# A fused attention and MoE kernel on one core: its third attention unit cut into two query chunks, with MoE work between them

## The chip, the core and the metric

The kernel runs on one core of a Trainium2 chip. The core has a matrix engine, TensorE (PE in the profile, with its weight loads as PEld), which writes to eight PSUM banks; a vector engine (DVE); an activation engine (ACT); GpSimd (POOL); and a queue engine, SyncE (SP), that issues DMAs. Each engine works through its own instructions in the order of the program and waits for others by semaphores. The metric is the device time of one execution in microseconds (us), the median of several; the profile is of one further execution.

## The reference

```python
def _attn_ref(q, k, v, g_q, g_k):            # q, k, v: 8 batches, 12 heads, 448 rows, 64
    def rmsnorm(x, g):
        rms = np.sqrt(np.mean(x * x, axis=-1, keepdims=True) + 1e-06)
        return x / rms * g
    q_n, k_n = (rmsnorm(q, g_q), rmsnorm(k, g_k))
    scale = 1.0 / np.sqrt(q.shape[-1])
    scores = scale * np.matmul(q_n, k_n.transpose(0, 1, 3, 2))
    scores = scores - np.max(scores, axis=-1, keepdims=True)
    attn = np.exp(scores)
    attn = attn / (np.sum(attn, axis=-1, keepdims=True) + 1e-09)
    return np.matmul(attn, v).astype(np.float32)

def _moe_ref(x, w_in, w_out):                # 3584 x 768, 768 x 2048, 2048 x 768
    h = x @ w_in
    g = np.maximum(0.01 * h, h)
    return (g @ w_out).astype(np.float32)

# the attention's output, heads side by side, is the x of the second part
```

All inputs and the output are float32; the kernel computes its matmuls in float16.

## The kernel before

A *unit* is four heads of one batch; a batch has three, and there are 24. Units are numbered from 0, and units 0 to 2 make batch 0. For a unit, q and k are loaded, squared (`prep_sq` on ACT or `prep_sqp` on POOL), summed (`prep_ssq`, DVE), turned into reciprocal roots (`prep_rinv`, ACT), normed (`prep_norm`, DVE), transposed by PE into PSUM and copied (`tr`, `trn`, `prep_tr`). Scores come in seven steps of keys (`qk`: four matmuls of 448 queries on four quarters of the array), each followed by one `ex` on ACT over 896 elements per partition. The exponent's shift is the largest score of the step 0 (`shift_max`, `shift_mm`). Then PE forms the denominators (`zsum`) and the sums with v (`pv`); `zinv` is the reciprocal on ACT, and `xmul` writes the unit's part of x to `xts`, on DVE.

```python
    def score(u, t, banks):
        for r in range(2):
            for a in range(2):
                nc.tensor.matmul(banks[a][64 * r:64 * r + 64, 0:S].rearrange("p (t x) -> p t x", t=NS),
                                 kT(u, r, a, t), qT(u, r, a), start=True, stop=True)
    def zsum(u, t0=0, t1=NS):
        s = st[u]
        for t in range(t0, t1):
            for r in range(2):
                for a in range(2):
                    nc.tensor.matmul(s["zt"][r][64 * a:64 * a + 64, 0:S], ones16[64 * r:64 * r + 64],
                                     s["et"][64 * r:64 * r + 64, t, a], start=(t == 0), stop=(t == NS - 1))
    def xmul(u):
        # ...
        for r in range(2):
            nc.vector.tensor_tensor(xts[b][:, g, r], s["pv"][r][:, 0:S], s["rz"][:, r], op=ALU.mult)
            drop(s["pv"][r])
    def moe1(b, ft):
        xt = xts[b]
        hps = aux([P, 512], FP32, "hps")
        for kt in range(KT):                  # KT = 6: two for each of the batch's three units
            nc.tensor.matmul(hps[:, 0:S], win16[:, kt // 2, kt % 2, ts(ft, P)], xt[:, kt // 2, kt % 2],
                             start=(kt == 0), stop=(kt == KT - 1))
        prelu(b, gt[:, ft, 64 * (b % 2):64 * (b % 2) + S], hps[:, 0:S])
        drop(hps)
```

The first MoE matmuls of a batch (`moe1`, 16 tiles of 128 columns of w_in) need all three units of it. PSUM holds two *slots* of two banks each (scores, in turn with denominators) and four single banks (`aux`). A queue of MoE items feeds PE inside the later units: `push(b)` adds those of batch b, and `fill` takes some at each step of the loop over units 3 to 23, so many that the queue lasts until the next batch. Before the loop there is an opening, written out by hand. `warm(n, bank)` issues n matmuls on a constant, whose result nobody reads. Its parts that the change touches, of units 0 to 2:

```python
        qk(0, (2,)); ex(0)                    # one statement a line in the kernel
        warm(8, wb)
        qk(0, (3,))
        tr(1, 0, ((ALL, acopy),))             # q of unit 1: transposes, copy on ACT
        tpk = tr(1, 1, ((K0, vcopy),))        # k of unit 1: first block, copy on DVE
        ex(0)
        qk(0, (4,)); ex(0)
        tr(1, 1, ((K1, vcopy),), tpk)         # k's other six blocks
        score0(1); shift_max(1); shift_bank(1)
        warm(10, st[1]["pb"])
        qk(0, (5,)); ex(0)
        warm(8, st[1]["pb"])
        qk(0, (6,)); ex(0)
        shift_mm(1)
        prep_ssq(2)
        ex(1); qk(1, (1,)); ex(1)
        zsum_slot(0); pv(0); prep_rinv(2); zinv(0); prep_norm(2)
        # ... loads, squares on POOL
        qk(1, (2,)); ex(1); trn(2, 0, vcopy)
        qk(1, (3,)); ex(1); trn(2, 1, vcopy)
        xmul(0)
        qk(1, (4,)); ex(1); qk(1, (5,)); ex(1)
        score0(2); shift_max(2)
        qk(1, (6,)); ex(1)
        shift_bank(2); warm(12, st[2]["pb"]); shift_mm(2)
        prep_ssq(3)
        ex(2); qk(2, (1,)); ex(2)
        zsum_slot(1); pv(1); prep_rinv(3); zinv(1); prep_norm(3)
        # ... loads, squares on POOL
        qk(2, (2,)); ex(2)
        trn(3, 0, vcopy); trn(3, 1, vcopy)
        xmul(1); prep_ssq(4)
        qk(2, (3,)); ex(2); qk(2, (4,)); ex(2)
        st[2]["zt"] = [aux([P, 512], FP32, "zt") for r in range(2)]
        sums(2, 0, 3)                         # zsum and pv of steps 0 to 2
        qk(2, (5,)); ex(2); sums(2, 3, 4)
        qk(2, (6,)); ex(2)
        prep_rinv(4); sums(2, 4, 5)
        qk(3, STEPS[0])
        sums(2, 5, NS)
        zinv(2); shift_max(3); xmul(2)
        push(0)
        first = slot()
        moe1_part(0, first, 0, KT - 2)        # two tiles of moe1, units 0 and 1
        shift_mm(3); ex(3)
        moe1_part(0, first, KT - 2, KT - 1); moe1_part(0, first, KT - 1, KT)
        # ... their two activations
        del queue[0:2]
        for u in range(3, NU):                # the loop
```

Of the kernel before, what the change touches and what calls it, by code (L numbers as in the profile page):

```python
# [13 lines left out]
ts = bass.ts  # L14
# [4 lines left out]
def kernel(  # L19
# [50 lines left out]

    ident16 = cst.tile([P, P], FP16)
# [98 lines left out]

    def prep_tr(u, ti, copies):
        tp = aux([P, NS, P], FP16, "tp")
        for (lo, hi), copy in copies:
            for x in range(lo, hi):
                nc.tensor.transpose(tp[:, x, :], buf(u, "n16")[:, ti, x].rearrange("p a d -> p (a d)"), ident16)
            copy(buf(u, "qkT")[:, ti, lo:hi], tp[:, lo:hi], ti == 0)

# [27 lines left out]
    def ex(u):  # L205
        s = st[u]
        if "et" not in s:
            s["et"] = epool.tile([P, NS, 2, S], FP16, tag="et", name="et")
        for t, sT in s["sT"]:
            if isinstance(sT, list):  # L210
                for a in range(2):
                    nc.scalar.activation(s["et"][:, t, a], sT[a][:, 0:S], AF.Exp, bias=s["eb"], scale=1.0)
            else:
                nc.scalar.activation(s["et"][:, t], sT[:, :, 0:S], AF.Exp, bias=s["eb"], scale=1.0)  # L214

# [23 lines left out]
    def shift_mm(u):  # L239
# [6 lines left out]
        else:  # L246
# [4 lines left out]
            nc.vector.tensor_reduce(s["spare"][:, 510:511], pb[:, 0:P], axis=AXL.X, op=ALU.max)  # L251
        s["eb"] = small.tile([P, 1], FP32, tag="eb", name="eb")
# [7 lines left out]
    def zsum(u, t0=0, t1=NS):  # L260
        s = st[u]
        for t in range(t0, t1):
            for r in range(2):
                for a in range(2):
                    nc.tensor.matmul(s["zt"][r][64 * a:64 * a + 64, 0:S], ones16[64 * r:64 * r + 64],
                                     s["et"][64 * r:64 * r + 64, t, a], start=(t == 0), stop=(t == NS - 1))

    def zsum_slot(u):
        s = st[u]
        s["zslot"] = slot()  # L270
        s["zt"] = [s["zslot"][:, r] for r in range(2)]
        zsum(u)
# [49 lines left out]
    def zinv(u):  # L322
        s = st[u]
        s["rz"] = zpool.tile([P, 2, S], FP32, tag="rz", name="rz")
        if "zslot" in s:
            nc.scalar.activation(s["rz"], s["zslot"][:, :, 0:S], AF.Ln)
            nc.scalar.activation(s["rz"], s["rz"], AF.Exp, bias=0.0, scale=-1.0)
        else:
            for r in range(2):
                nc.scalar.activation(s["rz"][:, r], s["zt"][r][:, 0:S], AF.Ln)  # L330
                nc.scalar.activation(s["rz"][:, r], s["rz"][:, r], AF.Exp, bias=0.0, scale=-1.0)

    def pv(u, t0=0, t1=NS):
# [3 lines left out]
        for t in range(t0, t1):  # L337
            for r in range(2):
                for a in range(2):
                    nc.tensor.matmul(s["pv"][r][64 * a:64 * a + 64, 0:S], vts[u % NV][64 * r:64 * r + 64, a, t],  # L340
                                     s["et"][64 * r:64 * r + 64, t, a], start=(t == 0), stop=(t == NS - 1))

    def xmul(u):
# [4 lines left out]
        for r in range(2):  # L348
            nc.vector.tensor_tensor(xts[b][:, g, r], s["pv"][r][:, 0:S], s["rz"][:, r], op=ALU.mult)  # L349
# [8 lines left out]
    def moe1(b, ft):  # L358
# [6 lines left out]
        drop(hps)  # L365

# [143 lines left out]

    HK = KT // 2
# [135 lines left out]
    def push(b):  # L647
# [3 lines left out]
        items = [(1.13, lambda ft=ft: (flush(), moe1(b, ft))) for ft in order]  # L651
        half = [(slice(0, 4)), (slice(4, 8))]
# [91 lines left out]
    with tc.manual_schedule():  # L744
# [12 lines left out]
        warm(42, wbank)  # L757
        prep_sq(0, CA, (0,))
# [5 lines left out]
        nc.vector.tensor_copy(gcol, gps[:, 0:1])  # L764
        prep_ssq(0, ALL, (1,))
# [6 lines left out]
        def tr(u, ti, chunks, tp=None):  # L772
            if tp is None:
                tp = aux([P, NS, P], FP16, "tp")
            for c, copy in chunks:
                for x in range(*c):
                    nc.tensor.transpose(tp[:, x, :], buf(u, "n16")[:, ti, x].rearrange("p a d -> p (a d)"), ident16)
                copy(buf(u, "qkT")[:, ti, c[0]:c[1]], tp[:, c[0]:c[1]], ti == 0)
            return tp
# [3 lines left out]
        tpk = tr(0, 1, ((K0, vcopy),))  # L783
# [40 lines left out]
        warm(8, wb)  # L824
        qk(0, (3,))
        tr(1, 0, ((ALL, acopy),))
        tpk = tr(1, 1, ((K0, vcopy),))
# [3 lines left out]
        tr(1, 1, ((K1, vcopy),), tpk)  # L831
# [3 lines left out]
        warm(10, st[1]["pb"])  # L835
        qk(0, (5,))
        ex(0)
        warm(8, st[1]["pb"])
        qk(0, (6,))
        ex(0)  # L840
        shift_mm(1)
        prep_ssq(2)
# [22 lines left out]
        xmul(0)  # L865
        qk(1, (4,))
        ex(1)
        qk(1, (5,))
        ex(1)
        score0(2)  # L870
        shift_max(2)
        qk(1, (6,))
        ex(1)
        shift_bank(2)
        warm(12, st[2]["pb"])
        shift_mm(2)
        prep_ssq(3)
        ex(2)
        qk(2, (1,))
        ex(2)  # L880
# [4 lines left out]

# [6 lines left out]
        qk(2, (2,))  # L892
        ex(2)
        trn(3, 0, vcopy)
        trn(3, 1, vcopy)
        xmul(1)
        prep_ssq(4)
        qk(2, (3,))
        ex(2)
        qk(2, (4,))  # L900
        ex(2)
        st[2]["zt"] = [aux([P, 512], FP32, "zt") for r in range(2)]
        sums(2, 0, 3)
        qk(2, (5,))
        ex(2)
        sums(2, 3, 4)
        qk(2, (6,))
        ex(2)
        prep_rinv(4)
        sums(2, 4, 5)  # L910
        qk(3, STEPS[0])
        sums(2, 5, NS)
        zinv(2)
        shift_max(3)
        xmul(2)
        push(0)
        first = slot()
        moe1_part(0, first, 0, KT - 2)
        shift_mm(3)
        ex(3)  # L920
        moe1_part(0, first, KT - 2, KT - 1)
        moe1_part(0, first, KT - 1, KT)
        for ft in range(2):
            prelu(0, gt[:, ft, 0:S], first[:, ft, 0:S])
        del queue[0:2]
# [120 lines left out]
```

## Time and profile before

| what | value |
|---|---|
| time, median of 3 | 421.84 us (421.16 to 421.97) |
| profiled execution, first to last instruction | 420.3 us |
| ACT busy, ex over 896 elements | 159.4 us, 1010 ns each, 166 of them |
| PE, first MoE matmuls | 120.8 us, 600 of them |
| PE, scores | 53.2 us, 664 matmuls |
| DMA | 62.42 MB, mean 149 GB/s |

The page of a profile gives for each engine the time in which it was busy and the number of instructions, then the span in 40 equal slices, where each digit is the busy share in tenths. A row of a timeline has start, length, engine, line of the kernel, what was written and read, and how many instructions were merged. The chain of waits follows the end of the execution back to what released each step. A busy PE is not PE at its peak: rows of fillers and half-speed matmuls count as busy too. A granted clock of 1.00 is full speed.

### The profile page before, as it was taken

How to read it: one execution, taken by the hardware profiler on the slowest of the kernel's cores; microseconds unless marked ns; L12 is line 12 of the kernel's file. 1: busy time of each engine (PE TensorE's matmuls, PEld its weight loads, DVE VectorE, ACT ScalarE, POOL GpSimd, SP SyncE). 2: the span in 40 equal slices, each digit the busy share in tenths (PEclk: the TensorE clock that was granted, in tenths of full speed). 3: DMA queues.
4: the chain of work that ended last, by engine and by line, in shares of the span. 5: the costliest groups of instructions: out<-in, count | busy, mean ns of one | idle time of the engine just before them, and what ended most of it. 6: DMA issues, size and time to landing. Idle time of an engine off the chain costs nothing.

```text
span 420.3 us, 9568 instructions
## 1 busy us (share of the span) xinstructions
PE 404.4 (96%) x3959; PEld 222.9 (53%) x3959; DVE 269.2 (64%) x440; ACT 303.6 (72%) x474; POOL 83.0 (20%) x75
## 2 busy tenths in 40 slices
PE   7977999999999999999999999999999999999995
PEld 6544444555445544555445544455445557558853
DVE  5788665787658736466448745467338787527762
ACT  5999878868987689867986779967986657653600
POOL 1958422300020111210121111120101101010000
PEclk9699999999999999999999999999999999999999
DMA  8999999889664795678565796578562460032023
GB/s 257 218 239 237 235 250 147 200 156 215 169 153 68 224 212 120 168 163 180 152 130 107 194 203 150 151 141 170 180 111 44 121 155 11 7 78 75 2 53 100
DMA packets 71951, 62.42 MB, mean 149 GB/s; under 512 B 36324, under 2 KB 67044, under 8 KB 71908
## 3 DMA queue, kind: packets, MB, share of 16 engines
q1 hardware_dynamic: 61312, 49.62, 47.2%
q0 software_dynamic: 10272, 11.80, 18.1%
q8 instruction: 31, 0.51, 0.5%
q10 hardware_dynamic: 324, 0.39, 0.3%
q14 instruction: 12, 0.10, 0.1%
HBM read 45.61 MB, written 11.01 MB: 135 GB/s over the span
## 4 chain that ended last, share of the span: by engine, by line
PE 83%; ACT 8%; DVE 6%; issue 1%; DMA 1%; SPq 0%; DVEq 0%; ACTq 0%
PE hps L362 27%; PE sT L195 8%; PE sT L340 6%; PE ma L444 5%; PE md L444 5%; PE mc L444 5%; ACT et L214 5%; PE bank L444 5%; PE bank L564 4%; PE op L403 3%; PE zc L283 3%; PE mb L444 3%; DVE n L167 2%; PE sT L444 2%; PE bank L403 1%
## 5 line engine op out<-in xcount | busy, mean ns | idle before, releaser
L214 ACT ACTIVATE et<-sT,eb 128x896 f16<-128x896 f32 x166 | 159.4, 1010 | 18.6 <-PE sT L195 16.9
L362 PE MATMUL hps<-xt,win 128*128 128x448 f16 x600 | 120.8, 353 | 0.2 <-DVE xt L349 0.2
L362 PEld LDWEIGHTS <-win 128*128 128x128 f16 x612 | 56.8, 98 | 58.2 <-issue 9.6
L320 POOL TENSOR_TENSOR xt<-x,rz 128x896 f16<-128x896 f32 x16 | 33.4, 2085 | 148.0 <-DMA rz<-zs 139.5
L356 ACT ACTIVATE gt<-hps 128x448 f16<-128x448 f32 x100 | 54.0, 556 | 6.1 <-PE hps L362 5.4
L167 DVE TENSOR_TENSOR n<-rq,rinv 128x896 f16<-128x896 f32 (+2 forms) x25 | 27.2, 1090 | 47.0 <-ACT rinv L161 44.2
L195 PE MATMUL sT<-qkT 64*64 64x448 f16 x664 | 53.2, 369 | 3.0 <-ACT et L214 1.9
L155 DVE TENSOR_REDUCE ssq<-sq 128x14 f32<-128x896 f32 (+2 forms) x49 | 50.3, 1058 | 1.6 <-ACT sq L144 1.6
L444 PEld LDWEIGHTS <-sa 128*128 128x128 f16 x352 | 32.8, 98 | 26.3 <-issue 6.1
L295 ACT COPY x<-sT 128x896 f32<-128x896 f32 x19 | 17.2, 906 | 36.4 <-DVE sT L245 36.4
L124 POOL DMA_DIRECT2D vt<-in_v_dram x24 | 18.2, 757 | 114.9 <-PE sT L340 107.4
L444 PEld LDWEIGHTS <-gt 128*128 128x128 f16 x264 | 25.2, 98 | 18.7 <-issue 2.1
L195 PEld LDWEIGHTS <-qkT 64*64 64x64 f16 x672 | 15.2, 105 | 36.8 <-issue 33.5
L340 PE MATMUL sT<-et,vt 64*64 64x448 f16 x532 | 28.5, 350 | 0.3
L403 PE MATMUL op<-wout,gt 128*128 128x384 f16 x160 | 28.4, 327 | 0.0
L232 DVE TENSOR_REDUCE sT<-sT 128x1 f32<-128x896 f32 x22 | 24.1, 1093 | 4.3 <-PE sT L195 4.3
L340 PEld LDWEIGHTS <-vt 64*64 64x64 f16 x672 | 20.7, 107 | 11.3 <-issue 1.7
L167 DVE TENSOR_TENSOR n<-rk,rinv 128x896 f16<-128x896 f32 (+2 forms) x26 | 26.1, 1009 | 0.0
L403 PEld LDWEIGHTS <-gt 128*128 128x128 f16 x192 | 17.6, 98 | 14.3 <-issue 3.0
L444 PE MATMUL ma<-wout,gt 128*128 128x384 f16 x128 | 23.5, 326 | 0.0
L425 DVE TENSOR_TENSOR sa<-gt 128x512 f16<-128x512 f16 (+1 forms) x15 | 8.2, 544 | 18.5 <-ACT gt L356 13.9
L144 ACT ACTIVATE sq<-rq 128x896 f32<-128x896 f32 (+2 forms) x18 | 16.3, 913 | 1.3 <-DMA rq<-in_q_dram 1.3
(135 smaller groups left out, 516.6 us busy)
## 6 DMA issues: line engine op xcount, KB each, us to landing
rq<-in_q_dram SPq DMA_DIRECT2D x24, 448.0 KB, 3.9
rk<-in_k_dram SPq DMA_DIRECT2D x24, 448.0 KB, 5.6
out_dram<-ost SPq DMA_DIRECT2D x52, 192.0 KB, 3.3
rz<-zs SPq DMA_DIRECT2D x76, 112.0 KB, 2.3
vt<-in_v_dram POOLq DMA_DIRECT2D x24, 224.0 KB, 5.1
win<-in_moe_w_in_dram POOLq DMA_DIRECT2D x8, 384.0 KB, 16.8
wout<-in_moe_w_out_dram POOLq DMA_DIRECT2D x2, 1536.0 KB, 29.7
out_dram<-ost SPq DMA_DIRECT2D x4, 96.0 KB, 2.1
```

The source lines that it names most:

```text
L124: nc.gpsimd.dma_start(vts[u % NV].rearrange("p a t d -> p a (t d)"), rows(v, u))
L155: nc.vector.tensor_reduce(buf(u, "ssq")[:, ti, :, c[0]:c[1]], buf(u, f"sq{ti}")[:, :, c[0]:c[1]], axis=AXL.X, op=ALU.add)
L167: nc.vector.tensor_tensor(buf(u, "n16")[:, ti, c[0]:c[1]].rearrange("p s a d -> p a s d"), src[:, :, c[0]:c[1]], buf(u, "rinv")[:, ti, :, ...
L195: nc.tensor.matmul(banks[a][64 * r:64 * r + 64, 0:S].rearrange("p (t x) -> p t x", t=NS), kT(u, r, a, t), qT(u, r, a), start=True, stop=True)
L214: nc.scalar.activation(s["et"][:, t], sT[:, :, 0:S], AF.Exp, bias=s["eb"], scale=1.0)
L232: nc.vector.tensor_reduce(s["spare"][:, 511:512], sT[:, :, 0:S], axis=AXL.XY, op=ALU.max)
L320: eng.tensor_tensor(xts[b][:, g], s["x32"], s["rz"], op=ALU.mult)
L340: nc.tensor.matmul(s["pv"][r][64 * a:64 * a + 64, 0:S], vts[u % NV][64 * r:64 * r + 64, a, t], s["et"][64 * r:64 * r + 64, t, a], start=(t ...
L356: nc.scalar.activation(dst, src, AF.Prelu, bias=0.0, scale=1.0, alpha=0.01)
L362: nc.tensor.matmul(hps[:, 0:S], win16[:, kt // 2, kt % 2, ts(ft, P)], xt[:, kt // 2, kt % 2], start=(kt == 0), stop=(kt == KT - 1))
L403: nc.tensor.matmul(op2[:, 0:HC], gt[:, ft, ds(col(t), P)], wout16[:, ft, ds(HC * half, HC)], start=(ft == 0), stop=(ft == FT - 1))
L444: nc.tensor.matmul(bank[:, 0:HC], a[:, f], b[:, f], start=(first and f == 0), stop=(f == HF - 1), skip_group_check=not first)
```

## The change

Three things are changed in the opening; the loop is the same apart from the shape of batch 0's first MoE items.

First, unit 1's order: its q copy goes from ACT to DVE; the transposes of k's later blocks go behind score 5, and their copy behind the shift; some filler is left out. Second, unit 2 is worked in two chunks of queries, 256 (`QA`) and 192 (`QB`): scores, exps, denominators, sums, reciprocal and multiply of the first come ahead of the second's, and MoE matmuls on the first chunk go between, two tiles of w_in to one bank (`moe1_two`). Score 0 of unit 2, which the shift needs, is made for all queries in two spare banks and then once more by chunk. Third, unit 3's transposes and its score 0, also in spare banks, go ahead of the sums of the second chunk. For this the four single banks are held in a list from the beginning (`hold`) and given back by hand (`drop`). It is meant to give PE useful work, and not filler or waits, before the loop begins. The core of the diff:

```diff
+    def score_c(u, steps, c):
+        n = 64 * (c[1] - c[0])
+        sT = slot()
+        for i, t in enumerate(steps):
+            for r in range(2):
+                for a in range(2):
+                    nc.tensor.matmul(sT[64 * r:64 * r + 64, a, n * i:n * i + n].rearrange("p (t x) -> p t x", x=64),
+                                     kT(u, r, a, t), qT(u, r, a)[:, c[0]:c[1]], start=True, stop=True)
+        st[u]["sT"] = (steps, sT)
 ...
+    def moe1_two(b, f, c, k0=0, k1=KT, bank=None):
+        n = 64 * (c[1] - c[0])
 ...
+        for i in range(2):
+            for kt in range(k0, k1):
+                nc.tensor.matmul(bank[:, n * i:n * i + n], win16[:, kt // 2, kt % 2, ts(f + i, P)], xts[b][:, kt // 2, kt % 2, cut(c)],
+                                 start=(i == 0 and kt == 0), stop=(kt == KT - 1), skip_group_check=True)
 ...
+        if b == 0:
+            items = [(w, lambda f=f, c=c: (flush(), moe1_two(b, f, c))) for w, c in ((1.28, QA), (0.96, QB)) for f in range(0, FT, 2)]
 ...
-        warm(8, wb)
+        warm(6, wb)
+        drop(wb)
         qk(0, (3,))
-        tr(1, 0, ((ALL, acopy),))
-        tpk = tr(1, 1, ((K0, vcopy),))
+        tr(1, 0, ((ALL, vcopy),))
+        tpk = tr(1, 1, ((K0, vcopy),), None, False)
         ex(0)
         qk(0, (4,))
         ex(0)
-        tr(1, 1, ((K1, vcopy),), tpk)
         score0(1)
         shift_max(1)
         shift_bank(1)
-        warm(10, st[1]["pb"])
         qk(0, (5,))
         ex(0)
-        warm(8, st[1]["pb"])
+        tr(1, 1, ((K1, None),), tpk, False)
         qk(0, (6,))
         ex(0)
+        warm(6, st[1]["pb"])
         shift_mm(1)
+        vcopy(buf(1, "qkT")[:, 1, 1:NS], tpk[1][:, 1:NS])
+        drop(tpk[0])
         prep_ssq(2)
 ...
-        xmul(0)
+        xmul(0, (0,))
         qk(1, (4,))
-        ex(1)
-        qk(1, (5,))
         ex(1)
         score0(2)
         shift_max(2)
+        qk(1, (5,))
+        ex(1)
         qk(1, (6,))
         ex(1)
         shift_bank(2)
-        warm(12, st[2]["pb"])
+        warm(8, st[2]["pb"])
         shift_mm(2)
 ...
         prep_ssq(3)
-        ex(2)
-        qk(2, (1,))
-        ex(2)
+        xmul(0, (1,))
+        score_c(2, (0, 1), QA)
+        ex_c(2, QA)
+        score_c(2, (2, 3), QA)
+        ex_c(2, QA)
         zsum_slot(1)
         pv(1)
         prep_rinv(3)
         zinv(1)
         prep_norm(3)
 ...
-        (steps 2 to 6 of unit 2, its sums, score 0 of unit 3, two tiles of moe1)
+        score_c(2, (4, 5), QA)
+        ex_c(2, QA)
+        xmul(1)
+        st[2]["zt"] = [aux([P, 512], FP32, "zt") for r in range(2)]
+        zsum(2, 0, 4, cut(QA))
+        score_c(2, (6,), QA)
+        ex_c(2, QA)
+        zsum(2, 4, NS, cut(QA))
+        pv(2, 0, NS, cut(QA))
+        zinv(2, cut(QA))
+        score_c(2, (0, 1), QB)
+        ex_c(2, QB)
+        score_c(2, (2, 3), QB)
+        ex_c(2, QB)
         trn(3, 0, vcopy)
         trn(3, 1, vcopy)
+        xmul(2, (0, 1), cut(QA))
+        first = moe1_two(0, 0, QA, 0, KT - 2)
+        score_c(2, (4, 5), QB)
+        ex_c(2, QB)
+        score0(3)
+        shift_max(3)
+        moe1_two(0, 0, QA, KT - 2, KT, first)
+        score_c(2, (6,), QB)
+        ex_c(2, QB)
+        push(0)
+        del queue[0]
+        mo()                                  # the next item of the queue: f=2, QA
+        shift_mm(3)
         prep_ssq(4)
+        ex(3)
+        zsum_slot(2, cut(QB))
+        mo()                                  # f=4, QA
+        pv(2, 0, NS, cut(QB))
+        zinv(2, cut(QB))
         prep_rinv(4)
+        xmul(2, (0, 1), cut(QB))
+        held.clear()
```

The line in parentheses stands for the old statements shown above; comments on `mo()` are added here.

## The prediction

> **What bounds the kernel now.** I read the page's busy shares and slices first, then the totals of five stretches, then the chain of waits up to 60 us, then the timeline of each engine for 8 to 60 us. The lines "PE", "PE" and "PEclk" of the page:
>
> ```profile
> PE 404.4 (96%) x3959; PEld 222.9 (53%) x3959; DVE 269.2 (64%) x440; ACT 303.6 (72%) x474; POOL 83.0 (20%) x75
> ...
> PE   7977999999999999999999999999999999999995
> ...
> PEclk9699999999999999999999999999999999999999
> ```
>
> PE is idle for 420.3 - 404.4 = 15.9 us. By the totals of stretches, 46.0 - 36.8 = 9.2 us of it lie before 46 us and 120.0 - 115.4 = 4.6 us after 300 us. So from about 46 us on PE is the bound, and what the change can win lies before that. The stretches of the beginning (columns: stretch, length, busy PE, PEld, DVE, ACT, POOL with counts, clock, DMA share, GB/s):
>
> ```profile
> 10.00:22.00 12.00, 10.28 (x106) 6.36 (x107) 9.35 (x20) 11.06 (x17) 10.33 (x14) 0.72 1.02 224
> 22.00:31.00 9.00, 7.11 (x119) 4.46 (x122) 7.73 (x13) 8.54 (x12) 5.01 (x6) 1.00 1.16 237
> 31.00:38.00 7.00, 5.38 (x96) 3.03 (x89) 6.26 (x9) 6.28 (x10) 5.91 (x7) 1.00 1.12 238
> 38.00:45.00 7.00, 5.87 (x71) 2.97 (x68) 5.33 (x10) 5.33 (x10) 3.88 (x3) 1.00 1.16 235
> 45.00:57.00 12.00, 11.63 (x101) 5.59 (x103) 7.55 (x9) 10.99 (x18) 4.26 (x4) 1.00 1.14 242
> ```
>
> ACT is nearly full up to 38 us, and part of PE's busy time there is filler (the "warm" matmuls). In 38 to 45 us no engine is full: a chain. From the chain of waits (start, length, what):
>
> ```profile
> 18.34 3.59 ACT et L214 x4
> ...
> 24.37 2.10 DVE n L167 x2
> ...
> 31.22 1.16 ACT et L212 x2
> ...
> 43.27 0.58 ACT rz L331
> 43.86 0.02 issue
> 43.88 0.64 DVE xt L349
> 44.52 0.04 issue
> 44.56 0.54 PE sT L370 x2
> 45.10 2.27 PE hps L362 x12
> ```
>
> Reciprocal of unit 2 on ACT, its multiply on DVE, then the first full MoE matmuls: only from 44.94 us (start of that row in the timeline) does PE have a queue of work that waits for nobody.
>
> **What the Trainium skill says.** (1) "TensorE: Matmul & The Clock Gate", Back-to-back issue gap: N / 2.4 + 2.5 ns for a warm matmul. The trace agrees: 12 matmuls of 448 columns in 2.28 us are 190 ns each. (2) Same page, Part 1: a window of 3.413 us decides between half and full clock. The trace has full clock from 4.7, half from 11.5 and full from 18.4 us on: steps of 6.83 us, twice the window. This matters because the change removes filler. (3) "ScalarE: Activation LUTs", What ACT_TABLE_LOAD costs: 0.833 ns per element, neighbours overlap. The trace agrees: four activations of 896 take 3.69 us, and one takes 1.0, so they follow at 0.90; two of 448 follow at 0.55 to 0.58. From those I estimate 1.0 us for 1024 elements, 0.79 for 768, 0.59 for 512, 0.48 for 384.
>
> **The change part by part, as a hand schedule.** Durations are those of the timeline rows.
>
> *Unit 1's order.* The copy of q's transposes leaves ACT (1.01 us, which began after a 0.48 wait) for DVE (0.68). So exp 3 and 4 of unit 0 run from 16.85 to 18.65 instead of 18.23 to 20.0. Score 0 of unit 1 can run at about 18.0 (before 18.52), since only k's first block is copied ahead of it. Its maxima (1.14 + 0.16 + 0.29 on DVE) end at about 20.05 instead of 20.77, the shift about 20.75 instead of 21.57. ACT ends exp 6 at about 20.7, so unit 1's exps begin near 20.8 instead of 21.79: 1.0 us won. But DVE then copies k's other blocks (0.56) and only then forms unit 2's sums of squares (2.07): these end at 23.35, before at 23.55. ACT, which wants them next, waits from 22.8. Of the 1.0 us some 0.4 remain: norm 2 starts near 23.95 instead of 24.37, exp 2 of unit 1 at 25.64 instead of 26.03.
>
> *Half of unit 0's multiply behind the maxima.* It takes 0.55 us of DVE out of the line between the copies and unit 2's maxima. Score 0 of unit 2 goes ahead of score 5. Maxima start at 27.85 instead of 28.72, the shift is there near 30.2 instead of 31.17, and ACT's five exps end at 30.15. So unit 2's exps start at 30.2 instead of 31.22: 1.0 us, and ACT's 0.61 us idle there goes. Unit 3's sums end at 32.25 (33.15), its norm starts at 32.85 (33.81). The gain is 0.95 us here.
>
> *Unit 2 in chunks.* Exps are 3 x 1.0 + 0.59 for 256 queries and 3 x 0.79 + 0.48 for 192: 6.4 us, as before (2 x 0.55 + 6 x 0.9 = 6.5). Score 0 is made twice: 0.2 us of PE. First chunk: two exps 30.2 to 32.2, uu/rinv and unit 1's reciprocal to 34.7, exps 4-5 and 6 to 36.2, denominators 0.25 us behind, Ln, Ln, Exp (0.28 + 0.37 + 0.64) to about 37.9. Second chunk's first two exps to 39.45. DVE meanwhile copies unit 3's transposes (0.68 + 0.62, ready near 39.1) and multiplies the first chunk (2 x 0.35) to 39.8. So MoE matmuls on units 0 and 1 (8 x 0.109 = 0.87) can run at 38.2 and those on unit 2 at 39.8, and not at 41.94 and 44.56. The score of exps 4-5 stands behind the first 0.87, which costs ACT about 0.2 us.
>
> *Tail of the opening.* Score 0 of unit 3 needs the bank that the multiply frees: 39.9; its maxima end near 41.5; MoE pair f=2 (1.31) runs under them to 41.7; shift to 42.4; unit 3's first exps (1.1) to 43.5 after that pair's activation; second chunk's denominators (28 x 0.083 / 4 = 0.58), pair f=4 (1.31), sums (0.58) bring PE to 44.1. Its reciprocal ends near 45.3.
>
> *Balance.* PE enters the loop at 44.1 instead of 44.94, 0.84 us. It has done three pairs of 256 queries, 3 x 1.31 = 3.9 us, where before it had done two tiles, 12 x 0.19 = 2.3: another 1.6. Sum 2.4 us. Against it: halves of a 448-matmul cost 109.2 + 82.5 = 191.7 ns, not 189.2, on 96 pairs: 0.24 us. And a wait on weights, next.
>
> ```profile
> L103 POOL DMA_DIRECT2D win<-in_moe_w_in_dram x8: 626/628/679, 13.1 to 23.1; - x8
> DMA to landing us min/median/max: 7.4/16.8/23.0
> ```
>
> The last part of w_in is issued at 23.1 and lands up to 23.0 us later: 46.1. Pair f=8 needs it, and the new order reaches f=8 at 44.1 + 1.3 = 45.4, the old order tile 8 only near 55. PE waits 0.6 us there. The norm of unit 4 also comes later (its sums of squares move from 38.2 to about 42.4, so norm at 46 instead of 44.8), and its transposes may hold PE 0.2 us. From a net 2.4 - 0.24 - 0.6 - 0.2 = 1.4 at worst, up to 2.1 where these waits replace idle time that PE has anyway (it waits 0.37 us for ACT at 53.46). I take 1.7: 421.84 - 1.7 = 420.1 us. After that PE is full (10.00 of 10 us in most stretches), so the gain reaches the end.
>
> **Rivals.** *The clock falls.* Filler goes from 8 to 6, from 10 + 8 to 6 and from 12 to 8. By columns streamed at 2.4 per ns, PE was about 36% active in the 3.41 us before it fell to half clock at 11.5 (14 transposes and 6 fillers at 0.053 and a score step at 0.187: 1.25 us), and 44% in 25.2 to 28.6 (14 transposes, 4 score steps: 1.5 us), where it kept full clock; after the change I count 43% in 18.4 to 21.8. A half-clock stretch there would make unit 0's sums last 5.2 instead of 2.6 us and cost 2 us or so: 422 to 423. Likewise the clock may rise at 21.8 instead of 18.4, which costs about 0.5: 420.6. For it: filler was put there for a reason; against it: 43% lies nearer the case that held. I give 1 in 6. *Weights by DMA become the bound.* DMA's share is 1.16 in 22 to 45 us; as the skill's "DMA: Bandwidth & Descriptors", Issuing engines are not separate DMA queues, says, all issuers share 16 engines, which this trace shows as long landings (wout 25.6 to 33.9 us). If unit 5's loads, now 0.4 us earlier, push w_in to 47 or 48, PE waits 1 to 2 us at f=8: 421 to 421.5. *Nothing arrives:* norm 4 late by 1.2 us puts unit 4's transposes, at the head of PE's order, into the way: 421.5. *More is won:* if all waits hide, 2.4 us, 419.4.
>
> **Range and chances.** The centre is 420.1. Misjudged hand-overs add about 0.7 either way, the clock up to 2.5 on the slow side. Eight times in ten: 418.9 to 422.0. 2% is 8.4 us, more than all of PE's idle time before 46 us could plausibly give; slower by 8.4 us would need several half-clock stretches. So 0.01 faster, 0.98 within, 0.01 slower.
>
> **What would show it.** Right: no q copy on ACT near 17.3; ACT waiting near 22.8 for the sums of squares; unit 2's exps near 30.2; first MoE matmuls near 38; PE waiting for w_in before f=8 at about 46; the loop's u=4 reached about 1 us earlier with less left in the queue. Wrong: a clock of 0.5 anywhere after 18.4; f=8 after 47; PE idle for unit 4's norm by more than 0.5 us; idle time that appears after 60 us.

## The result and the profile after

| | before | after | ratio, 95% |
|---|---|---|---|
| time, median | 421.90 us (421.16 to 422.53, 4 runs) | 424.86 us (423.94 to 425.53, 4 runs) | 1.0069, 1.0044 to 1.0094 |
| profiled execution | 420.3 us | 423.7 us | |

The change makes the kernel 3.0 us slower. The prediction was 420.1 us, with a range of 418.9 to 422.0. The profiled execution of the changed kernel is the slowest of its four (425.53 us), so its profile shows some half a microsecond more than the median.

The page of the changed kernel, its busy times, the slices of PE and those of the granted clock:

```profile
PE 406.5 (96%) x4125; PEld 232.1 (55%) x4125; DVE 270.7 (64%) x445; ACT 304.0 (72%) x475; POOL 82.8 (20%) x75
...
PE   7887999989999999999999999999999999999996
...
PEclk9589999999999999999999999999999999999999
```

PE's busy share is 96% as before. New are the ninth of its digits, 8 where before had 9 (84.7 to 95.3 us), and the second and third digits of the clock: 5 and 8 where before had 6 and 9. The same five stretches of the opening as in the prediction (stretch, length, busy PE, PEld, DVE, ACT, POOL with counts, clock, DMA share, GB/s):

```profile
10.00:22.00 12.00, 9.84 (x88) 5.59 (x92) 9.47 (x19) 10.66 (x16) 10.17 (x14) 0.56 1.02 224
22.00:31.00 9.00, 8.03 (x111) 4.18 (x111) 7.27 (x11) 7.91 (x12) 4.95 (x6) 0.83 1.14 247
31.00:38.00 7.00, 4.89 (x113) 3.49 (x116) 6.18 (x9) 6.49 (x9) 5.53 (x6) 1.00 1.12 251
38.00:45.00 7.00, 6.54 (x131) 4.94 (x130) 4.02 (x11) 5.36 (x10) 1.95 (x2) 1.00 1.15 260
45.00:57.00 12.00, 11.75 (x147) 8.83 (x142) 8.60 (x11) 10.31 (x19) 6.60 (x6) 1.00 1.15 227
```

The clock is 0.56 and 0.83 in the first two (0.72 and 1.00 before): half speed lasts from 11.4 to 25.1 us, and before it lasted from 11.5 to 18.4.

To see where the time goes I compare the moment at which each unit's shift is formed on DVE, the same instruction in every kernel. The table holds that moment minus that of before, in us, also for six of the experiments below (one profile each):

| unit | before, at | after | e1 | e2 | e3 | e4 | e9 | e12 |
|---|---|---|---|---|---|---|---|---|
| 0 | 12.88 | -0.28 | -0.32 | -0.17 | -0.34 | -0.05 | -0.14 | -0.34 |
| 3 | 44.74 | +0.01 | -1.59 | -1.43 | -1.33 | -0.02 | -1.43 | -0.46 |
| 4 | 59.71 | +1.71 | +0.11 | +0.27 | +0.38 | -0.03 | +0.27 | -0.46 |
| 5 | 73.98 | +1.43 | -0.76 | -0.01 | -0.50 | +1.27 | -0.61 | -0.46 |
| 6 | 87.11 | +2.46 | -0.75 | +1.03 | -0.50 | +2.31 | -0.60 | -0.46 |
| 9 | 132.88 | +3.23 | -0.17 | +1.03 | -0.50 | +2.31 | -0.60 | -0.45 |
| 11 | 163.62 | +3.52 | -0.17 | +1.33 | -0.50 | +2.66 | -0.60 | -0.23 |
| end | 420.26 | +3.47 | -0.22 | +1.29 | -0.54 | +2.59 | -0.20 | -0.29 |

The row of unit 0 stands before anything that the change moves, so 0.3 us of a row is chance of the single execution. The clock differs too: it stood at half for 6.8 us of the opening in before, e3, e4, e9 and e12, for 13.7 in after, for 3.4 in e2, and never in e1. Units 4 and 5 can't be read alone, because the kernels have then done different amounts of queue work; from unit 6 on the amounts agree. The loss of after is complete by unit 11: 2.46 us by unit 6, 0.77 between 7 and 9, 0.29 by 11. The 0.29 comes with unit 9, whose last step has one item instead of two: e2 and e4, with the same numbers of items there, lose 0.30 and 0.35 between units 9 and 11, and e1 and e3, with those of before, nothing.

By unit 6 it has three parts. PE enters the loop at 47.14 us instead of 44.94, with 5 pairs of 256 queries and 8 of 192 left instead of 14 tiles: 5 x 1.31 + 8 x 0.99 = 14.47 us instead of 14 x 1.135 = 15.89. That is 2.20 - 1.42 = 0.78 us. The second part is new idle time of PE. Its timeline around 75 and 85 us, of the changed kernel (start, length, engine, line, operation, tiles, instructions, and in brackets idle time and what ended it):

```profile
74.88 1.46 PE L452 MATMUL op<-wout,gt 128*128 128x384 f16 x8
76.37 0.38 PE L201 MATMUL sT<-qkT 64*64 64x448 f16 x4
77.28 0.38 PE L201 MATMUL sT<-qkT 64*64 64x448 f16 x4 [0.53 <-ACT et L221]
...
84.51 0.38 PE L201 MATMUL sT<-qkT 64*64 64x448 f16 x4
85.40 1.52 PE L374 MATMUL sT<-et,vt 64*64 64x448 f16 x28 [0.51 <-ACT et L221]
86.85 0.85 PE L316 MATMUL zc<-et,onesr 128*32 128x224 f16 x28
88.38 0.22 PE L271 MATMUL sT<-dg,onesp 128*128 128x64 f16 x2 [0.67 <-DVE dg L261]
```

And the same two places of the kernel before:

```profile
73.45 2.77 PE L403 MATMUL op<-wout,gt 128*128 128x384 f16 x16
76.14 0.57 PE L195 MATMUL sT<-qkT 64*64 64x448 f16 x8
...
80.76 2.77 PE L403 MATMUL op<-wout,gt 128*128 128x384 f16 x16
83.46 0.38 PE L195 MATMUL sT<-qkT 64*64 64x448 f16 x4
```

The op rows are second MoE matmuls, 8 of them to an item of the queue. Before has two items in unit 5's first step and two in its last, after has one in each. With one item PE is through after 1.46 us. Its next scores then wait for an exp on ACT (0.53), and at the end of the unit the sums wait for one (0.51) and the shift for DVE (0.67): 1.71 us. Against that, some 0.5 us of shorter waits that before had earlier in the loop are gone. The totals from PE's entry into the loop to unit 6's shift, of before and of after:

```profile
44.94:87.11 42.17, 41.09 (x425) 20.66 (x424) 29.64 (x39) 31.59 (x48) 13.29 (x11) 1.00 1.00 201
47.14:89.57 42.43, 40.08 (x500) 26.64 (x497) 30.38 (x41) 30.38 (x48) 14.47 (x13) 1.00 0.83 182
```

PE's idle time grows from 1.08 to 2.35 us, by 1.27. The third part is that PE's busy time falls by 1.01 us only and not by the 1.42 that is left out of the queue: 0.41. 0.78 + 1.27 + 0.41 = 2.46, as the table says.

### The profile page after: what moved, and what is told of

Its sections match the earlier page's. It is cut to its first block, busy times and chain, and to the rows that moved or that the text cites. A ratio compares the mean times of both kernels' runs of the same rounds, so it can differ in the third digit from the quotient of the medians.

```text
span 423.7 us, 9910 instructions
## 1 busy us (share of the span) xinstructions
PE 406.5 (96%) x4125; PEld 232.1 (55%) x4125; DVE 270.7 (64%) x445; ACT 304.0 (72%) x475; POOL 82.8 (20%) x75
## 4 chain that ended last, share of the span: by engine, by line
PE 80%; DVE 7%; ACT 5%; DMA 3%; issue 3%; POOL 1%; SPq 0%; DVEq 0%; ACTq 0%; POOLq 0%
PE hps L396 24%; PE sT L201 8%; PE sT L374 5%; PE bank L493 5%; PE md L493 5%; PE bank L614 4%; PE ma L493 4%; PE mc L493 4%; PE op L452 4%; ACT et L221 4%; PE hps L407 3%; PE zc L316 3%; PE mb L493 2%; DVE n L168 2%; DMA vt<-in_v_dram 2%
## 5 line engine op out<-in xcount | busy, mean ns | idle before, releaser
L221 ACT ACTIVATE et<-sT,eb 128x896 f16<-128x896 f32 x159 | 152.7, 1009 | 19.4 <-PE sT L201 18.9
L396 PE MATMUL hps<-xt,win 128*128 128x448 f16 x516 | 103.6, 353 | 0.0
L396 PEld LDWEIGHTS <-win 128*128 128x128 f16 x528 | 49.2, 98 | 50.1 <-issue 8.2
L353 POOL TENSOR_TENSOR xt<-x,rz 128x896 f16<-128x896 f32 x16 | 33.2, 2078 | 150.3 <-DMA rz<-zs 124.3
L168 DVE TENSOR_TENSOR n<-rq,rinv 128x896 f16<-128x896 f32 (+2 forms) x25 | 26.3, 1055 | 48.8 <-ACT rinv L162 46.8
L201 PE MATMUL sT<-qkT 64*64 64x448 f16 x636 | 51.0, 373 | 3.6 <-DVE qkT L780 1.8
L390 ACT ACTIVATE gt<-hps 128x448 f16<-128x448 f32 x86 | 46.5, 556 | 4.4 <-PE hps L396 3.8
L493 PEld LDWEIGHTS <-gt 128*128 128x128 f16 x264 | 25.2, 98 | 18.4 <-issue 1.8
L201 PEld LDWEIGHTS <-qkT 64*64 64x64 f16 x648 | 14.0, 105 | 35.6 <-issue 29.7
L259 DVE TENSOR_REDUCE sT<-sT 128x1 f32<-128x896 f32 x21 | 22.9, 1092 | 4.3 <-PE sT L201 4.2
L407 PEld LDWEIGHTS <-win 128*128 128x128 f16 x192 | 16.5, 98 | 4.3 <-issue 1.9
```

The source lines that it names most:

```text
L168: nc.vector.tensor_tensor(buf(u, "n16")[:, ti, c[0]:c[1]].rearrange("p s a d -> p a s d"), src[:, :, c[0]:c[1]], buf(u, "rinv")[:, ti, :, ...
L259: nc.vector.tensor_reduce(s["spare"][:, 511:512], sT[:, :, 0:S], axis=AXL.XY, op=ALU.max)
L353: eng.tensor_tensor(xts[b][:, g], s["x32"], s["rz"], op=ALU.mult)
L390: nc.scalar.activation(dst, src, AF.Prelu, bias=0.0, scale=1.0, alpha=0.01)
L407: nc.tensor.matmul(bank[:, n * i:n * i + n], win16[:, kt // 2, kt % 2, ts(f + i, P)], xts[b][:, kt // 2, kt % 2, cut(c)], start=(i == 0 an ...
L493: nc.tensor.matmul(bank[:, 0:HC], a[:, f], b[:, f], start=(first and f == 0), stop=(f == HF - 1), skip_group_check=not first)
```

## The experiments

**The number of items per step.** The loop takes items by a running account:

```python
        debt[0] += total * WD[d] / left       # total: weight of the queue; left: weight of the steps to come
        while queue and debt[0] >= queue[0][0] * 0.5:
            # ... run the next item, and take its weight off debt[0]
```

At the loop's start the queue's weight is 14 x 1.13 + 12 x 1.31 = 31.54 before and 5 x 1.28 + 8 x 0.96 + 12 x 1.31 = 29.8 after. So the account rounds differently. Items in the four steps of units 3, 4, 5 and 6:

```
before  2212  2212  2112  2122
after   2112  2222  1211  2122
```

e1_pattern gives the changed kernel before's numbers from unit 5 on:

```diff
         debt[0] += total * WD[d] / left
+        debt[0] = {(4, 2): 0.6, (4, 3): 1.5, (5, 0): 2.213}.get((u, d), debt[0])
```

> The changed kernel, with the number of MoE items at the steps of units 4 and 5 put back: the debt of the queue is set so that from unit 5 on every step takes as many items as in the kernel before (in the changed kernel steps 0 and 3 of unit 5 take one item where the kernel before takes two, and so does step 3 of unit 9). Theory A (the items fall on other steps, and where a step at the end of a unit has only one, PE waits for the maxima or for ACT): the four gaps of PE after 60 us that the kernel before has not (at 76.8, 84.9, 87.7 and 134.8 us, 2.4 us together) go, about 2.1 us less than the changed kernel, 422.7 us. Theory B (all of the loss is the half clock from 18.2 to 25.1 us): no difference, 424.8 us. Theory C (the small shapes of the chunks cost more on PE and that is all of it): no difference.

Measured: 421.72 us, ratio to before 1.0007 (0.9992 to 1.0021); the changed kernel without this edit took 424.86. PE's timeline at the same two places of e1:

```profile
72.69 2.76 PE L452 MATMUL op<-wout,gt 128*128 128x384 f16 x16
...
82.92 1.49 PE L374 MATMUL sT<-et,vt 64*64 64x448 f16 x28
...
85.16 0.22 PE L271 MATMUL sT<-dg,onesp 128*128 128x64 f16 x2
```

Sixteen matmuls in the first step again, and no bracket in these rows: the waits are gone.

e4_before_pattern does the reverse. It is the kernel before with the numbers of after from the end of unit 4 on, and nothing of the change otherwise:

```diff
         debt[0] += total * WD[d] / left
+        debt[0] = {(4, 3): 3.0, (5, 0): 1.659}.get((u, d), debt[0])
```

> The kernel before, its opening untouched, with the changed kernel's numbers of items from step 3 of unit 4 on (three items there, then one at step 0 and one at step 3 of unit 5, one at step 3 of unit 9). Theory A: the same gaps of PE appear here too, and the time grows by about 2.1 us, to 424.0 us. Theories B and C: no difference, 421.9 us, as neither the opening nor a shape is changed.

Measured: 424.55 us, ratio 1.0059 (1.0045 to 1.0073), 2.8 us more than before (421.75 in these runs). PE's timeline of e4:

```profile
77.12 0.38 PE L195 MATMUL sT<-qkT 64*64 64x448 f16 x4 [0.52 <-ACT et L214]
...
85.25 1.52 PE L340 MATMUL sT<-et,vt 64*64 64x448 f16 x28 [0.51 <-ACT et L214]
...
88.23 0.22 PE L244 MATMUL sT<-dg,onesp 128*128 128x64 f16 x2 [0.68 <-DVE dg L234]
```

These are after's three waits, of the same lengths, in a kernel that has no chunk and no changed order. By unit 6 it has lost 2.3 us, more than their sum of 1.71: PE's busy time from 44.94 us to that shift is also 0.54 us longer than before's (41.63 and 41.09), for which no run shows a cause. e1's recovery and e4's loss together show that the account alone makes and unmakes the larger part of the loss.

**The filler and the clock.** e2_filler puts filler back into the changed kernel and leaves the account as it is; e3_both is e2 and e1 together:

```diff
-        warm(6, wb)
-        drop(wb)
+        warm(8, wb)
 ...
+        warm(3, wb)
+        drop(wb)
         score0(1)
 ...
-        warm(6, st[1]["pb"])
+        warm(16, st[1]["pb"])
         shift_mm(1)
 ...
-        warm(8, st[2]["pb"])
+        warm(12, st[2]["pb"])
         shift_mm(2)
```

> The changed kernel with filler put back in the opening: 8 and not 6 before score 3 of unit 0, 3 new ones in the gap of PE before unit 1's first score (17.4 us), 16 and not 6 before unit 1's shift, 12 and not 8 before unit 2's. Nothing else is moved. Theory B (the clock): the granted clock is back at full speed at 18.2 us and not at 25.1, unit 2's exps start near 30.3 and not at 31.65, and the time falls by 1.3 to 1.5 us, to 423.4 us; the gaps after 60 us stay. Theory A (the pattern of items alone): the clock may rise earlier, but the time stays at 424.8 us, since the PE gaps after 60 us are the loss.

> Both edits together, the pattern of items of the kernel before and the filler put back. If A and B are two separate losses they add up: 424.8 - 2.1 - 1.4 = 421.3 us, just under the kernel before. If they are one loss seen twice, about 422.7 us. What is then left against my prediction of 420.1 would be theory C, the cost of the small shapes, some 1 us.

Measured: e2 424.14 us, 1.0047 (1.0033 to 1.0062); e3 421.66 us, 0.9997 (0.9989 to 1.0004). The account costs 2.5 us from e3 to e2, and 3.1 from e1 to after. The filler brings 0.7 us from after to e2, where the runs overlap (four of 423.94 to 425.53, five of 423.33 to 424.47), and only 0.1 from e1 to e3. The medians hide what happens: e1's fourteen runs fall in two groups by mean granted clock. Four at 0.983 to 0.987 took 422.8 to 423.8 us, ten at 0.994 to 1.0 took 421.0 to 422.6. Of the 18 runs with after's filler (after and e1), seven have a mean clock below 0.988; of the 108 runs of the nine kernels with e2's filler, none has, and none of e3's 21 is below 0.992. So the filler does keep the clock from the long stretch at half. PE's timeline of after, where the clock decides:

```profile
16.83 0.59 PE L201 MATMUL sT<-qkT 64*64 64x448 f16 x4
17.70 0.59 PE L201 MATMUL bank<-qkT 64*64 64x448 f16 x4 [0.28 <-DVE qkT L780]
...
22.23 2.83 PE L298 MATMUL sT<-et,ones 64*64 64x448 f16 x28
```

And of e3:

```profile
16.99 0.59 PE L201 MATMUL sT<-qkT 64*64 64x448 f16 x4
17.51 0.43 PE L795 MATMUL bank<-onesp 128*128 128x128 f16 x3
17.87 0.38 PE L201 MATMUL bank<-qkT 64*64 64x448 f16 x4
...
21.52 1.49 PE L298 MATMUL sT<-et,ones 64*64 64x448 f16 x28
```

In after PE is idle for 0.28 us at 17.4 us, there is less filler behind it, and the clock stays at half for 13.7 us instead of 6.8: unit 0's denominators last 2.83 us instead of 1.49. In e3 three fillers stand in that gap, and the scores behind them already take 0.38 us. The Trainium skill, "TensorE: Matmul & The Clock Gate", What's actually happening, calls the clock's window free-running, so that the moment of the change varies; that fits kernels whose runs fall into two groups, though no run here shows the window itself. The profile of e1 fits too: its opening is after's, instruction for instruction, and PE even waits longer at that place:

```profile
17.61 0.38 PE L201 MATMUL bank<-qkT 64*64 64x448 f16 x4 [0.64 <-DVE qkT L781]
```

Yet its granted clock is 1.00 from 10 to 31 us; it never fell at 11.4. So that wait alone does not decide. That less filler makes the long stretch at half likelier is shown by the counts of runs; which of the four places where e2 puts filler back matters was not tested.

**The shapes.** e3 has the account and the clock of before, and still no gain. I suspected the halved matmuls: merged rows of the chain gave 2.73 us for 24 of 256 columns and 2.09 for 24 of 192, against 2.28 for 12 of 448, which would be 0.13 us for each two tiles, 1.0 in all. Three kernels were to show it. e6_before_small is the kernel before with the fourteen tiles of batch 0 in the loop as 7 + 7 pairs in chunks, at the same numbers of items, with `moe1_two` taken over from the changed kernel:

```diff
+        if b == 0:
+            items = items[0:2] + [(w, lambda f=f, c=c: (flush(), moe1_two(b, f, c))) for w, c in ((1.28, QA), (0.96, QB)) for f in range(2, FT, 2)]
 ...
+        debt[0] = {(3, 0): 2.2, (3, 1): 2.2, (3, 2): 1.0, (3, 3): 2.2, (4, 0): 1.7, (4, 1): 1.7, (4, 2): 0.7, (4, 3): 1.7, (5, 0): 2.213}.get((u, d), debt[0])
```

> The kernel before with its opening and with the number of items at each step kept, but the fourteen tiles of batch 0 that the loop works are cut into seven pairs of 256 and seven of 192 queries, as in the changed kernel. Theory C: 7 x 0.14 = 1.0 us more than the kernel before, 422.7 us. If the shapes cost what I predicted: 0.2 us more, 421.95 us.

Measured: 422.17 us, 1.0009 (1.0002 to 1.0017): 0.4 us by the ratio. Two rows of its timeline, with the rows that follow them:

```profile
47.72 2.78 PE L373 MATMUL hps<-xt,win 128*128 128x256 f16 x24
50.43 0.57 PE L195 MATMUL sT<-qkT 64*64 64x448 f16 x8
...
62.98 2.15 PE L373 MATMUL hps<-xt,win 128*128 128x192 f16 x24
65.06 0.57 PE L195 MATMUL sT<-qkT 64*64 64x448 f16 x8
```

And of the kernel before:

```profile
48.60 2.43 PE L362 MATMUL hps<-xt,win 128*128 128x448 f16 x12
50.96 0.57 PE L195 MATMUL sT<-qkT 64*64 64x448 f16 x8
```

From the start of a row to that of the next it is 2.71 and 2.08 us, and 2.36 for the whole tiles. Half of 2.71 + 2.08 is 2.40, so two tiles cost 0.04 us more in chunks, 16 tiles 0.3. My 1.0 came from comparing rows that included the hand-over to the scores with one that didn't. The records of single matmuls say the same: they follow each other at 109.2, 82.5 and 189.2 ns, as the prediction had it. The suspicion falls.

e5_full_tiles (e3 with three pairs of each chunk and then ten whole tiles) and e10_six_tiles (five pairs and six whole tiles) were made to win that 1.0 us back. Both are the e3 kernel with this (the lambda is left out and the comments are added here), and new account values:

```diff
-            items = [(w, ...) for w, c in ((1.28, QA), (0.96, QB)) for f in range(0, FT, 2)]
+            items = [(w, ...) for w, c in ((1.28, QA), (0.96, QB)) for f in range(0, 6, 2)]    # e10: 10
+            items += [(1.13, lambda ft=ft: (flush(), moe1(b, ft))) for ft in range(6, FT)]     # e10: 10
```

> The changed kernel with filler and pattern put back (as e3_both), and of batch 0's first MoE items only the first three pairs (six tiles of w_in) in chunks of 256 and 192 queries; the other ten tiles go as whole 448-query matmuls again, at steps of the same number of items. Theory C (each pair of tiles in chunks takes 1.37 + 1.05 us of PE, read from e3_both's trace, against 2 x 1.14 whole, 0.14 us more): five pairs fewer are worth 0.7 us, 421.0 us. If the shapes cost what I predicted (0.03 us a pair): 421.5 us, no difference from e3_both's 421.66 that can be measured.

> e3_both with the last six tiles of w_in as whole 448-query matmuls (five pairs in chunks ahead of them), in e3_both's number of items at each step; the second chunk's items stand behind the first's, and no item of batch 1 is drawn forward, which is what spoiled e5_full_tiles (PE waits of 0.88 us at 46.3 and 2.28 us at 98.3 us). Theory C, 0.14 us a pair: three pairs, 0.4 us less, 421.25 us, unless ACT holds units 3 and 4, where the shorter items then only lengthen PE's waits: 421.7 us.

Measured: e5 429.49 us, 1.0171 (1.0149 to 1.0193); e10 422.21 us, 1.0002 (0.9992 to 1.0011). e5 tells nothing of the shapes. Its second-chunk pairs come at the start of the loop, where PE waits 0.88 us at 46.3 for the second chunk's multiply, and its queue is one item ahead, so that a tile of batch 1 waits 2.28 us at 98.3 for unit 5's multiply on DVE. e10 has neither fault, and gains nothing over e3, as the 0.04 us say. In its profile, though, it lies 0.1 us ahead of e3 up to unit 14 (-0.60 and -0.50 in the terms of the table, in an execution whose clock did not fall in the opening) and loses 0.8 us between units 14 and 15, to a meeting of DVE and POOL that the last section shows. e11 below loses 0.55 us at the same place in the same way. So what whole tiles would bring without it stays open.

**Where the opening's lead goes.** From unit 2's first exps to PE's entry into the loop, two windows of e3, divided where its first MoE matmuls start:

```profile
30.30:39.30 9.00, 6.59 (x162) 5.09 (x158) 6.36 (x9) 8.31 (x13) 7.62 (x7) 1.00 1.11 254
39.30:45.80 6.50, 6.49 (x110) 4.68 (x109) 5.21 (x11) 4.75 (x9) 1.15 (x1) 1.00 1.16 248
```

And of the kernel before, from 31.2:

```profile
31.20:40.20 9.00, 7.22 (x126) 4.04 (x119) 8.29 (x10) 8.00 (x12) 7.80 (x8) 1.00 1.12 237
40.20:44.94 4.74, 3.77 (x34) 1.77 (x34) 3.08 (x8) 3.56 (x9) 1.79 (x2) 1.00 1.17 237
```

The sums are 13.08 us busy of 15.50 in e3 and 10.99 of 13.74 before. PE's idle time in this stretch was to be filled; it falls from 2.75 to 2.42 us only. All but 0.01 of it now stands before 39.3, where ACT is busy for 8.31 of 9 us. The extra 1.66 us of MoE work (3 x 1.31 - 12 x 0.189) took 1.76 us of extra time. Four rows of e3's timeline of PE show what the first MoE matmuls stand behind:

```profile
35.99 0.41 PE L298 MATMUL bank<-et,ones 64*64 64x256 f16 x8 [0.91 <-ACT et L240]
...
37.44 0.53 PE L229 MATMUL sT<-qkT 64*64 64x192 f16 x16
37.90 0.95 PE L180 MATMUL bank<-ident,n 128*128 128x128 f16 x14
39.31 0.27 PE L407 MATMUL bank<-xt,win 128*128 128x256 f16 x1 [0.46 <-DVE qkT L779]
```

They have unit 0's and unit 1's x from about 36.1 us, but the transposes of unit 3 come first in PE's order, and the bank that the MoE matmuls write is the one in which unit 3's q transposes wait for their copy (0.46 us). e9_tr takes unit 3's q transposes ahead of the first chunk's last denominators, its k transposes behind them, and the first chunk's sums behind the second chunk's first scores. e8_earlier_tr does this on e5, e11_six_tiles_tr on e10:

```diff
+        trn(3, 0, vcopy)
         zsum(2, 4, NS, cut(QA))
-        pv(2, 0, NS, cut(QA))
+        trn(3, 1, vcopy)
         zinv(2, cut(QA))
 ...
-        trn(3, 0, vcopy)
-        trn(3, 1, vcopy)
-        xmul(2, (0, 1), cut(QA))
+        pv(2, 0, NS, cut(QA))
         first = moe1_two(0, 0, QA, 0, KT - 2)
+        xmul(2, (0, 1), cut(QA))
```

> As e5_full_tiles, and unit 3's transposes are put ahead of the first chunk's last denominators, its sums with v behind the second chunk's first two scores. In e3_both PE waits 0.46 us at 38.9 us before the first MoE matmuls, since their bank is that of unit 3's q transposes, which DVE copies until 39.3, and ACT then waits 0.83 us for the score of exps 4-5. If those waits are on the path: 0.7 to 0.9 us less than e5_full_tiles, 420.2 us. If PE's work alone decides from there on: no difference from e5_full_tiles, 421.0 us.

> e3_both (filler and pattern put back, 421.66 us) with unit 3's q transposes ahead of the first chunk's last denominators, its k transposes behind them, and the first chunk's sums with v behind the second chunk's first two scores. The bank of the first MoE matmuls is then free early, and the two waits of 0.46 us (PE, 38.9 us) and 0.83 us (ACT, 39.9 us) go. If they are on the path that sets the end: 0.5 to 0.8 us less, 421.0 us. If PE's own work alone decides from there on, only the 0.46: 421.2 us. If the loop is held by ACT and not by PE: no difference, 421.7 us.

> Both of the last two edits. If each acts by itself and PE's work is the bound: 420.6 us, better than the kernel before by 1.1 us. If ACT holds units 3 and 4: 421.5 us, and then the opening has nothing more to give.

Measured: e8 427.65 us, 1.0146 (1.0127 to 1.0164), with e5's faults; e9 421.41 us, 0.9986 (0.9977 to 0.9995); e11 421.88 us, 1.0000 (0.9990 to 1.0011). The two windows of e9:

```profile
30.50:39.20 8.70, 7.06 (x163) 5.11 (x161) 6.97 (x9) 7.99 (x13) 7.63 (x8) 1.00 1.11 253
39.20:45.70 6.50, 6.50 (x112) 4.75 (x110) 4.81 (x10) 5.08 (x10) 1.16 (x1) 1.00 1.16 250
```

The stretch is 15.20 us, 0.3 shorter than e3's, and PE's idle time 1.64 us instead of 2.42; its busy time is 0.48 longer. It has four more changes between whole-array and quarter-array matmuls, two each way (0.09 us each, see the last section), by estimate 0.3 to 0.4 of that. The first MoE matmuls still start at 39.19 us only: the order is freer, but the first chunk's sums now stand ahead of them. In time e9 is 0.25 us better than e3, about as much as the stretch, though the medians come from different sets of runs. It is the only form with the chunks that beats the kernel before, by 0.4 us in the medians.

**The order without the chunks.** e7_before_order is the kernel before with the new order of units 0 and 1 and the filler of e2, unit 2 undivided. In e12_order_banks the second half of unit 0's multiply also goes behind the first exps of unit 2. Its core, with comments added here:

```diff
-        tr(1, 0, ((ALL, acopy),))
+        tr(1, 0, ((ALL, vcopy),))
 ...
-        xmul(0)
+        xmul(0, (0,))
         qk(1, (4,))
         ex(1)
-        qk(1, (5,))
-        ex(1)
         score0(2)
         shift_max(2)
+        qk(1, (5,))
+        ex(1)
 ...
+        xmul(0, (1,))                         # e7: here
         ex(2)
+        xmul(0, (1,))                         # e12: here
```

> Only the mended order of units 0 and 1 (q's copy on DVE, k's later copy behind the shift, half of unit 0's multiply behind unit 2's maxima, score 0 of unit 2 ahead of score 5), with e2_filler's filler; from unit 2 on all is as in the kernel before: whole queries, whole tiles, its pattern. If the gain of the opening that I predicted for this part arrives (unit 2's exps at 30.3 and not at 31.2 us): 421.75 - 0.9 = 420.9 us, and the chunks were the part that cost. If the start of the loop is held by something else than this chain (ACT's idle time of 2 us in 36 to 45 us only grows): 421.7 us.

> As e7_before_order (only the order of units 0 and 1 is mended), but with the second half of unit 0's multiply behind unit 2's first exps in the program, so that unit 1's sums take banks that are free. In e7_before_order PE waited 0.91 us at 32.0 us for that multiply's bank, which ate the lead of unit 2. If the order gains what its trace showed at unit 2's shift (0.4 to 0.6 us net of the start): 421.7 - 0.5 = 421.2 us. If the opening's lead is taken back by the chain of reciprocal, multiply and MoE before the loop: 421.7 us.

Measured: e7 421.67 us, 0.9998 (0.9988 to 1.0008); e12 421.61 us, 0.9988 (0.9979 to 0.9998). In e7 PE waits 0.91 us at 32.0 for the bank that the second half of the multiply frees, and 0.75 at 144.2, of which more below. e12 has nothing of the first and 0.07 us of the second. Its interval and e9's overlap almost wholly: the chunks, with their own forms of scores, exps and MoE items, bring nothing that these runs can tell from the order alone.

## Why the prediction was wrong

- **Unit 1's order: right in its steps.** q's copy is off ACT, and ACT waits for unit 2's sums of squares, 0.40 us at 23.27 in e3 and 0.31 in after. Unit 2's exps start at 30.31 in e3 (predicted 30.2, before 31.22), but e3's whole profile begins 0.34 us early, so the lead is some 0.6 us and not 1.0. In after the clock takes it: 31.65.
- **"The clock falls": the rival came true, in another form.** It was placed at 18.4 to 21.8 as a late rise, at 0.5 us. In after's profile it rose a whole step later, at 25.1, and the stretch 18.4 to 25.1 ran at half speed; a clock of 0.5 after 18.4 was a sign of being wrong that the prediction had named. By the medians it is worth 0.7 us (after to e2), with overlapping runs; in e1 the two groups lie 1.7 us apart (means 423.3 and 421.6). The shares of PE's activity that the prediction weighed (36, 43 and 44%) do not decide it: e1, with the same opening as after, kept the full clock where before and after fell to half.
- **Small shapes: right.** 0.24 us was predicted; the single records give the predicted distances, and e6 0.4 (0.1 to 0.7).
- **Weights and unit 4's transposes: charged for nothing.** PE has no wait before f=8; the last part of w_in is issued at 22.4 us in after and lands 20.8 us later at most, at 43.2, where 46.1 had been taken from before.
- **The opening's idle time: the first step that failed.** "So MoE matmuls on units 0 and 1 ... can run at 38.2" came out at 39.31 in e3, and "PE enters the loop at 44.1" at 45.80. Between the two the prediction allowed 5.9 us and it took 6.49: the streams of MoE matmuls and denominators run at the predicted distances, but the eight changes between whole-array and quarter-array matmuls in this stretch, four each way, cost 0.09 us each, by estimate 0.7 in all, which the prediction had not counted. I had counted what work could run under ACT's waits, and not what stands ahead of it in PE's order: a transpose, its copy, its bank. PE enters the loop 1.7 us later than predicted, and the gain of 1.7 us shrank to about 0.1, e3's distance from before, which is within the noise.
- **"After that PE is full (10.00 of 10 us in most stretches), so the gain reaches the end": the step that made the kernel slower.** PE was full because the account gave each step the number of items that fills it. The change alters the queue's total, so the numbers fall otherwise, and waits of 1.7 us appear after 60 us; in time it costs 2.5 us (e3 to e2), 2.8 (before to e4) or 3.1 (e1 to after). The reading was too kind besides: of before's stretches of 10 us between 50 and 100 us one has PE busy for 10.00 and the others for 9.39 to 9.90; only from 100 to 300 us is it full (199.7 of 200). "Idle time that appears after 60 us" was among the prediction's signs of being wrong, but no step of it asks what could bring it about, though the weights 1.28 and 0.96 stand in the diff, and the item numbers follow from them by arithmetic.

From after by way of e2 and e3 to before, the 3.1 us between the medians are 0.7 of clock and 2.5 of account, less 0.1 gained by the opening. These parts add up by construction, and by way of e1 they are 3.1 of account and 0.1 of filler, so only the account's 2.5 to 3.1 us stand firm; how much of after's loss the clock makes depends on which runs are taken. Not settled is the rest of what the opening could give: PE still waits 1.64 us in e9's stretch, and no kernel here moves the first MoE matmuls to 36.1 us; in e3 the four single banks go to the denominators and sums of unit 2's first chunk at that time.

## What to carry to other kernels

Where work is dealt out by a running account, any change of a size or a weight deals all later work anew: recompute the number of items in each step before judging the change, and hold it fixed when measuring something else. Filler that looks idle may be what holds the clock, and its worth shows in the spread of the runs' clocks more than in a median. Idle time of an engine is not room for work until the work's place in that engine's order, and its bank, are free at that moment.

## What the runs showed of the hardware

**A small DVE operation can last five times as long beside one on POOL.** DVE's timeline of after, with three instructions that each form a difference of two fp16 tiles:

```profile
125.74 0.42 DVE L477 TENSOR_TENSOR sa<-sa,gt 128x512 f16<-128x512 f16 x1
...
127.54 2.26 DVE L480 TENSOR_TENSOR sa<-gt 128x512 f16<-128x512 f16 x1
129.72 0.41 DVE L483 TENSOR_TENSOR sa<-gt,sa 128x512 f16<-128x512 f16 x1
```

POOL's timeline at that time, of the same kernel:

```profile
127.45 2.07 POOL L353 TENSOR_TENSOR xt<-x,rz 128x896 f16<-128x896 f32 x1 [8.98 <-ACT et L221]
```

And PE's timeline of it some 8 us later:

```profile
135.52 0.22 PE L271 MATMUL sT<-dg,onesp 128*128 128x64 f16 x2 [0.71 <-DVE dg L261]
```

The operation starts 0.09 us after POOL's and ends 0.28 us after it: that fits an operation that waits for POOL to finish. DVE then waits for nothing up to the `dg` that PE waits for, and PE pays 0.71 us at 134.8. The Trainium skill, "SBUF — State Buffer", Who interferes with whom, describes it: a DVE instruction with two SBUF inputs and a GpSimd instruction that reads SBUF exclude each other for the whole instruction. Whether the two meet differs from kernel to kernel. In before the same instruction started 0.57 us before POOL's end and took 0.85 us at 125.1; in e1 it took 2.08 us at 124.3, PE waited 0.53, and unit 9's shift came 0.58 us later in the table; in e10 another of the three took 2.31 us at 220.4, beside 2.34 us of POOL, and PE waited 0.75; in e11 one took 2.04 us at 219.8, and PE waited 0.50; in e7 the wait at 144.2 follows a DVE operation of 2.53 us. So a shift of the loop by half a microsecond can cost or save 0.5 to 0.9 us far from the change. That the 0.77 us which after loses between units 7 and 9 are this one is read from the traces; no run took POOL's operation away.

**Changing between whole-array and quarter-array matmuls has a price.** In e3's single records the first quarter-array matmul starts 282 ns after a 448-column one instead of 189, 203 after a 256-column one instead of 109, and 176 after a 192-column one instead of 82.5: 0.09 us in each of these cases. The way back takes about as much: a whole-array matmul starts 282 ns after the last of four quarter-array ones of 448 columns, and 175 after those of 192. Work cut into more, shorter groups pays it more often.
